# Gated mix of local attention and a gMLP on one core: absolute sums over 1024 elements, two sums over x moved into the first exponential's wait, spatial products one tile later

## Chip, core and metric

The kernel runs on one core of a Trainium2 chip. The metric is the device time of one execution in microseconds (us). A core has five engines with a queue of instructions each: PE (matrix products), ACT (elementwise functions, copies, also out of PSUM), DVE (elementwise work on tensors, also out of PSUM), POOL (little work here) and SP (issues most DMAs). Every engine works its own queue in order; between engines, and towards DMAs, an instruction waits on semaphores.

## What is computed

x has 2048 rows of 1024. With `g = sigmoid(x · gate_w)` for each row, the output is `g·a + (1-g)·b`:

```
qkv = x @ wqkv                      # 32 heads of 32
a   = softmax over 8 keys at distances 0,2,..,14 of q·k, times v, @ wo
z   = gelu(x @ w_in)                # 3584 columns: z1 | z2
z2  = layernorm(z2)
b   = (z1 * (w_sp @ z2 + b_sp)) @ w_out
```

All inputs are bf16. 

## The kernel before

Five stages follow each other on PE, and PE's instructions are in the same order from the first to the last in both kernels. (1) Columns of z2 (`z2_tile`, line 302). (2) q, k and v (`plain_rows`, line 617, and `row_pair`, line 637); they go through DRAM. (3) The rest of z2, then z1 with its gelu (line 802). (4) The spatial product `w_sp @ z2`: `g_chunk` (line 829) for two column chunks of 14 tiles each, then `seven_products` (line 920), seven times, for the other half. (5) The output products with w_out and wo (lines 1048, 1127 and 1137).

`row_pair`, `seven_products` and `both_pairs` compute a two by two block product with seven products in place of eight (the scheme of Strassen and Winograd). It needs sums of blocks, which DVE makes: `x_sums[0..3]` from x (`x_block_sums`, lines 561 to 566), `t1..t4` from w_sp (`t_sums`), `sums[0..3]` from z2 (`s_sum`). These sums are kept in fp16, and scaled by powers of two so that they do not overflow. The powers come from sums of absolute values or maxima: `q_abs`, `row_sums`, and three that the change touches:

- line 412, over the attention output `obuf` at each of four stores (`store_o`): eight sums of 512 elements a partition, into `o_l1`;
- line 1016 (`v_sum`), over the products z1·g of the two chunks: 28 sums of 512, into `v_l1`;
- line 1012 (`u_sums`), over those of the other half: 28 sums of 512, into `u_l1`.

Each is an ACT instruction `Abs` with an accumulated output; the profile shows it as an ACTIVATE and an ACTIVATION_READ_ACCUMULATOR.

In `seven_products(n)` PE makes seven products of eight matmuls each, which this text counts 0 to 6. Between them ACT copies: line 943 (bank `pa` to bank `pb`, after product 0; product 2 needs it), 945 (`e5`, after product 1), 951 (`pb` to `pc`, after product 2; product 4, which writes `pb` again, waits for it), 777 twice (seeds of two banks for the next n), 956 (after product 3), 980 (after product 6). `extra(n, place)` hangs further work between the products: `v_sum` three times at place 1 and three times at place 5. `u_sums(n-1)` stands behind line 956.

In `g_chunk` PE makes a tile of 512 columns in 16 matmuls; ACT copies it into one of three slots `gsb` (line 833), and DVE multiplies it into `z1c` (line 836).

The attention itself runs on DVE beside PE, from stage 2 to the end of `g_chunk`: for each of 8 groups of heads the products q·k and their folds (lines 348 to 362), the largest of a window (`soft_a`, lines 369 to 375), the exponential on ACT (line 378), its sum and quotient (`soft_b`), and the products with v (lines 391 to 398) of the group before, which stand in the wait for the exponential. Group 0 has no group before it.

The order of the queues is written out when the program is built. `Beat` keeps a clock of PE's work (`beat.now`) and a heap of work that is due at a time (`beat.at`); `attention_steps` yields DVE steps with a time and a duration each. `beat.run` advances the clock after each product and issues what has become due. So the times in the code (lags, durations) only set places in the queues; on the chip an instruction starts when its queue and its semaphores let it. `top`, `top_b` and lines 494 to 513 (`whole_power`) turn a maximum into a power of two: a transposition on PE (line 503), a maximum on DVE (504), a broadcast on PE (506).

Of the kernel before, what the change touches and what calls it, by code (L numbers as in the profile page):

```python
# [10 lines left out]
F32 = mybir.dt.float32  # L11
# [4 lines left out]
P = 128  # L16
# [6 lines left out]
NG = NH // HG  # L23
# [34 lines left out]
def kernel(  # L58
# [64 lines left out]
    b_in = sm.tile([P, 8], BF, name="b_in")  # L123
    b_up = sm.tile([P, 8], BF, name="b_up")
    w_l1 = sm.tile([P, 7], F32, name="w_l1")
    v_l1 = s1[:, 0:28]
    u_l1 = sm.tile([P, 28], F32, name="u_l1")
    top = sm.tile([P, 1], F32, name="top")
    top_i = sm.tile([P, 1], I32, name="top_i")
    top_b = sm.tile([P, 1], BF, name="top_b")  # L130
# [269 lines left out]
    def load_qk(g):  # L400
        sync.dma_start(q_t, bass.AP(tensor=q_d.tensor, offset=q_d.offset + g * S * C, ap=[[NJ * C, P], [1, NJ * C]]))
        sync.dma_start(k_t, bass.AP(tensor=k_d.tensor, offset=k_d.offset + (g * (S + 16) + 2) * C, ap=[[NJ * C, P], [1, NJJ * C]]))
# [4 lines left out]
    def store_o(g):  # L407
        dst = o_d[:, (g - 1) * C:(g + 1) * C].rearrange("(p j) c -> p j c", j=NJ)
        sync.dma_start(dst, obuf)
        lag = 1.5 if g + 1 == NG else 12.0  # L410
        for k in range(8):
            beat.at(beat.now + lag + 1.8 * k, lambda k=k: nc.scalar.activation(  # L412
                abs_out.rearrange("p (j c) -> p j c", j=2), obuf[:, 2 * k:2 * k + 2, :], ACT.Abs,
                accum_out=o_l1[:, 4 * g - 4 + k:4 * g - 3 + k]))

    def attention_steps(t):
        beat.at(t - 11.0, lambda: load_qk(0))
        beat.at(t + 32.0, lambda: load_v(0))
        for g in range(NG):
            for took, fn in qk_steps(0) + qk_steps(1) + [(0.73, to_two), (0.73, to_one)]:  # L420
                yield t, took, fn
            t = beat.vector
            if g + 1 < NG:
                beat.at(t + 1.0, lambda g=g: load_qk(g + 1))
            if g == 0:
                t += 3.0
            else:
                for took, fn in pv_steps(g - 1, 0):
                    yield t, took, fn
                t = beat.vector  # L430
            yield t, 1.75, soft_a
            t = beat.vector
            beat.at(t + 1.0, soft_exp)
            if g == 0:
                t += 5.0
            else:
                for took, fn in pv_steps(g - 1, 1):
                    yield t, took, fn
                t = beat.vector
                if g + 1 < NG:  # L440
                    beat.at(t + 1.0, lambda g=g: load_v(g))
                else:
                    load_v(g)
                if g % 2 == 0:
                    beat.at(t + 1.5, lambda g=g: store_o(g - 1))
            yield t, 2.25, soft_b
            t = beat.vector
        for took, fn in pv_steps(NG - 1, 0) + pv_steps(NG - 1, 1):
            yield t + 5.0, took, fn
        t = beat.vector  # L450
        beat.at(t + 9.0, lambda: store_o(NG - 1))
# [104 lines left out]
    def x_block(half, e):  # L556
        return x_even_odd[:, 4 * half:4 * half + 4, :, e]

    def x_block_sums():
        v = nc.vector  # L560
        nc.scalar.activation(a22s, x_block(1, 1), ACT.Copy, scale=x_by)
        v.tensor_scalar(a21s, x_block(0, 1), x_by, None, ALU.mult)
        TT(x_sums[0], a22s, a21s, ALU.add)
        v.scalar_tensor_tensor(x_sums[2], x_block(0, 0), x_by, a21s, ALU.mult, ALU.subtract)
        v.scalar_tensor_tensor(x_sums[1], x_block(0, 0), x_by, x_sums[0], ALU.mult, ALU.subtract)
        v.scalar_tensor_tensor(x_sums[3], x_block(1, 0), x_by, x_sums[1], ALU.mult, ALU.add)

    def q_abs(k):
        nc.scalar.activation(abs_1024.rearrange("p (k c) -> p k c", k=KT), wg_slots[4 + k // 4][:, k % 4], ACT.Abs,
# [25 lines left out]
        next(q_steps)  # L595

    QK_US = NJ * KT * 2 * C * BEAT
    beat.steps = attention_steps(beat.now + QK_US + 13.0)

    def store_rows(st, ch, j0, nj, pos0, pos1):  # L600
        for pos in range(pos0, pos1):
# [209 lines left out]
            load_z1c(0)  # L811

    gs = [0]

    def g_chunk(c):
        wsp = wsp_slots[c]
        z1c = z1c_slots[c % 2]
        for f in range(NF):
            ps = seeded.pop(0)
            n = NF * c + f + AHEAD  # L820
            if n < 2 * NF:
                seed(bsp_bc[:, 512 * (n // NF):512 * (n // NF) + 512])
            elif n == 2 * NF:
                TT(bsp_more, bsp_bc[:, 1536:2048], bsp_bc[:, 1024:1536], ALU.subtract)
                beat.on_vector(0.7)
            elif n == 2 * NF + 3:
                seed_group()
            for i in range(16):
                nc.tensor.matmul(ps[:], z2[:, f, i, :], wsp[:, i, :, :].rearrange("p a t -> p (a t)"),  # L829
                                 start=False, stop=(i == 15), skip_group_check=True)  # L830
            gsb = gsb_slots[gs[0] % 3]
            gs[0] += 1
            nc.scalar.copy(gsb, ps[:])
            if c == 1 and f == NF - 1:
                t_sums(2)
            TT(z1c[:, f, :], gsb, z1c[:, f, :], ALU.mult)
            beat.on_vector(0.43)
            beat.run(16 * 512)

    def u_late(f):  # L840
        return u_first[:, f // 7] if f % 7 == 0 else z2[:, f - 1, 0:8, :]
# [49 lines left out]
    def t_sums(k):  # L891
        if k == 0:
            TT(t1, b_hi[:, 0:8], b_lo[:, 0:8], ALU.subtract)
        elif k == 1:
            TT(t3, b_hi[:, 8:16], b_hi[:, 0:8], ALU.subtract)
        elif k == 2:
            TT(t2, b_hi[:, 8:16], t1, ALU.subtract)
        else:
            TT(t4, b_lo[:, 8:16], t2, ALU.subtract)
        beat.on_vector(2.3)  # L900
# [31 lines left out]
    def seven_products(n, extra):  # L932
        fa, fb = n, n + 7
        for f in (fa, fb):
            sync.dma_start(u_late(f).rearrange("p (c a) q -> p c (a q)", c=2),
                           z1_d[2:4, :, f * 512:(f + 1) * 512].rearrange("c p t -> p c t"))
        more = n + 1 < 7
        e5 = e5_slots[n % 2]
        extra(n, 0)
        pa, pe = seeded.pop(0), seeded.pop(0)  # L940
        product(pa, z2[:, fa, 0:8, :], lambda k: b_lo[:, k])
        pb = bank()
        nc.scalar.copy(pb[:], pa[:])
        product(pe, sums[0], lambda k: t1[:, k])
        nc.scalar.copy(e5, pe[:])
        if more:
            s_sum(n + 1, 0)
        extra(n, 1)
        product(pb, sums[1], lambda k: t2[:, k])
        pc = bank()  # L950
        nc.scalar.copy(pc[:], pb[:])  # L951
        if more:
            seed_group()
        product(pa, z2[:, fa, 8:16, :], lambda k: b_lo[:, 8 + k])
        gsb = next_gsb()
        nc.scalar.copy(gsb, pa[:])
        if n:
            u_sums(n - 1)
        g_out(fa, 2, gsb)
        extra(n, 2)  # L960
        product(pb, sums[2], lambda k: t3[:, k])
        gsb = next_gsb()
        TT(gsb, pb[:], e5, ALU.add)
        beat.on_vector(0.7)
        g_out(fb, 3, gsb)
        extra(n, 3)
        product(pc, sums[3], lambda k: b_hi[:, 8 + k])
        if more:
            s_sum(n + 1, 2)
        gsb = next_gsb()  # L970
        TT(gsb, pc[:], e5, ALU.add)
        beat.on_vector(0.7)
        g_out(fa, 3, gsb)
        extra(n, 4)
        product(pb, z2[:, fb, 8:16, :], lambda k: t4[:, k])
        if more:
            s_sum(n + 1, 1)
            s_sum(n + 1, 3)
        gsb = next_gsb()
        nc.scalar.copy(gsb, pb[:])  # L980
        g_out(fb, 2, gsb)
        extra(n, 5)
# [22 lines left out]
            TT(w_t(f, 3), b21, w_t(f, 1), ALU.subtract)  # L1005
        beat.on_vector(0.43)

    def u_sums(n):
        for h, f in enumerate((n, n + 7)):
            for k in range(2):  # L1010
                c = 4 * n + 2 * h + k
                nc.scalar.activation(abs_out.rearrange("p (i q) -> p i q", i=4), u_late(f)[:, 4 * k:4 * k + 4, :], ACT.Abs,  # L1012
                                     accum_out=u_l1[:, c:c + 1])

    def v_sum(c, f):
        nc.scalar.activation(abs_out, z1c_slots[c][:, f, :], ACT.Abs, accum_out=v_l1[:, 14 * c + f:14 * c + f + 1])  # L1016

    def u_rows(q, r, half):
        if q < 4:
# [192 lines left out]
    def extra(n, place):  # L1212
# [8 lines left out]
        if place == 0:  # L1221
            for f in sum_sets.get(n, ()):
                for k in range(4):
                    w_sum(f, k)
        if place in (1, 5) and n < 5:
            for f in range(3 * n, min(14, 3 * n + 3)):
                v_sum(place // 4, f)
        if n == 5 and place == 0:
            nc.vector.tensor_reduce(top[:], v_l1, AX.X, ALU.max)
            next(v_steps)  # L1230
        if (n, place) in ((5, 3), (6, 0)):
            next(v_steps)
        if n == 2 and place == 5:
            nc.vector.tensor_reduce(top[:], o_l1[:], AX.X, ALU.max)
            next(o_steps)
        if (n, place) in ((3, 3), (4, 0)):
            next(o_steps)
# [41 lines left out]
    beat.at(t0 + 48.0, lambda: (nc.vector.tensor_reduce(top[:], wo_l1[:], AX.X, ALU.max), next(wo_steps)))  # L1279
    g_chunk(0)  # L1280
    g_chunk(1)
    for n in range(7):
        seven_products(n, extra)
    beat.flush(1e9)
# [2 lines left out]
    prepare(1)  # L1287
    mix_pair(0)
    wo_scale(1)
    u_sums(6)  # L1290
    for k in range(4):
        wo_sum(k)
    attn_pair(0)
# [37 lines left out]
```

## Time and profile before

| | |
|---|---|
| median of 3 runs | 690.11 us (689.65 to 690.2) |
| the profiled execution, its own time | 689.57 us |
| its span, first to last instruction | 687.4 us |
| PE busy | 679.3 us, 99% of the span |
| DVE busy | 564.6 us, 82% |
| ACT busy | 425.4 us, 62% |
| granted PE clock | 1.00 in every slice |

One execution is recorded; the 2.2 us between its time and its span lie before the first and after the last instruction. In the views "idle before" is the time that an engine stood still ahead of an instruction, and the arrow names what released it. A matmul of 512 columns is recorded as 379 ns, and the next one starts 216 ns after it: they overlap.

### The profile page before, as it was taken

What the parts mean: (1) busy time and instruction counts of PE and PEld (TensorE: products, weight loads), DVE (VectorE), ACT (ScalarE), POOL (GpSimd) and SP (SyncE); (2) the same over time, 40 slices, a digit from 0 to 9 for tenths busy, and PEclk for the clock granted to TensorE, in tenths of its full rate; (3) what the DMA queues carried; (4) which work ended last, traced back from release to release, by engine and by line L of the source; (5) the groups of instructions that cost most, each with busy time, mean ns of one, the idle gap of its engine ahead of it and who ended that gap; (6) DMA issues with size and microseconds to landing.
All of it is one profiled execution on the core that took longest, in us unless ns stands there. A gap on an engine that the chain in (4) does not pass through costs nothing.

```text
span 687.4 us, 9089 instructions
## 1 busy us (share of the span) xinstructions
PE 679.3 (99%) x3327; PEld 355.3 (52%) x3327; DVE 564.6 (82%) x701; ACT 425.4 (62%) x823; POOL 13.2 (2%) x45
## 2 busy tenths in 40 slices
PE   9999999999999999999999999999899999999997
PEld 4489666666654655444444444444344444444443
DVE  4649959999999997999998889994478888776653
ACT  4458767655566999759754997327987552223332
POOL 0000000000000022000000000000000000000000
PEclk9999999999999999999999999999999999999999
DMA  8995976554597308899978999918211413222210
GB/s 234 183 198 154 203 204 151 154 130 102 157 254 202 130 1 216 191 292 346 301 255 282 147 266 236 252 36 260 77 37 56 143 42 92 62 62 71 68 45 32
DMA packets 187996, 108.67 MB, mean 158 GB/s; under 512 B 146480, under 2 KB 172592, under 8 KB 187696
## 3 DMA queue, kind: packets, MB, share of 16 engines
q1 hardware_dynamic: 186224, 101.81, 57.1%
q10 hardware_dynamic: 1728, 6.29, 2.9%
q8 instruction: 26, 0.43, 0.2%
q14 instruction: 18, 0.15, 0.1%
HBM read 59.51 MB, written 34.41 MB: 137 GB/s over the span
## 4 chain that ended last, share of the span: by engine, by line
PE 95%; ACT 3%; DMA 1%; issue 0%; SPq 0%; DVE 0%; DVEq 0%; ACTq 0%
PE ps L617 16%; PE ps L302 14%; PE ps L829 14%; PE ps L802 14%; PE ps L1048 12%; PE ps L920 10%; PE ps L637 7%; PE ps L1137 6%; ACT arena L1016 1%; PE ps L1127 1%; ACT arena L412 1%; DMA arena<-in_B_w_in_dram 1%; ACT arena L1012 0%; PE po L506 0%; ACT ps L777 0%
## 5 line engine op out<-in xcount | busy, mean ns | idle before, releaser
L617 PE MATMUL ps<-arena 128*128 128x512 bf16 (+1 forms) x640 | 115.8, 337 | 0.0
L302 PE MATMUL ps<-arena 128*128 128x512 bf16 (+1 forms) x512 | 97.7, 353 | 0.2
L829 PE MATMUL ps<-arena 128*128 128x512 bf16 x448 | 97.7, 379 | 0.0
L617 PEld LDWEIGHTS <-arena 128*128 128x128 bf16 x640 | 83.1, 144 | 27.9 <-issue 0.5
L802 PE MATMUL ps<-arena 128*128 128x512 bf16 x448 | 97.0, 379 | 0.0
L1048 PE MATMUL ps<-arena 128*128 128x512 f16 (+1 forms) x392 | 92.8, 379 | 0.0
L920 PE MATMUL ps<-arena 128*128 128x512 bf16 (+1 forms) x392 | 85.9, 379 | 3.3 <-ACT ps L951 1.7
L302 PEld LDWEIGHTS <-arena 128*128 128x128 bf16 x512 | 50.1, 98 | 47.6 <-DVE arena L322 0.3
L348 DVE TENSOR_TENSOR arena<-arena 128x8192 bf16<-128x8192 bf16 x16 | 70.7, 4422 | 0.2
L802 PEld LDWEIGHTS <-arena 128*128 128x128 bf16 x448 | 43.7, 98 | 52.4
L391 DVE TENSOR_TENSOR arena<-arena,att_A 128x8192 bf16<-128x8192 bf16 x16 | 70.7, 4419 | 0.0
L829 PEld LDWEIGHTS <-arena 128*128 128x128 bf16 x448 | 43.5, 98 | 52.5 <-issue 0.5
L920 PEld LDWEIGHTS <-arena 128*128 128x128 bf16 (+1 forms) x392 | 38.0, 98 | 49.8 <-issue 4.4
L1048 PEld LDWEIGHTS <-arena 128*128 128x128 f16 (+1 forms) x392 | 38.3, 98 | 46.1
L623 ACT CAST arena<-ps 128x512 bf16<-128x512 f32 (+1 forms) x80 | 38.3, 508 | 32.1 <-PE ps L617 30.6
L351 DVE TENSOR_TENSOR arena<-arena 128x4096 bf16<-128x4096 bf16 (+1 forms) x32 | 56.2, 1755 | 0.8
L637 PE MATMUL ps<-arena 128*128 128x512 f16 (+1 forms) x224 | 52.4, 379 | 0.0
L307 ACT ACTIVATE arena<-ps 128x512 bf16<-128x512 f32 x64 | 34.2, 537 | 27.8 <-PE ps L302 27.8
L1137 PE MATMUL ps<-arena 128*128 128x512 f16 (+3 forms) x200 | 50.3, 375 | 0.0
L1117 DVE SCALAR_TENSOR_TENSOR arena<-ps,g_s,arena 128x512 bf16<-128x512 f32 (+2 forms) x33 | 24.0, 734 | 28.7 <-ACT arena L1169 19.9
L805 ACT ACTIVATE arena<-ps 128x512 bf16<-128x512 f32 x56 | 32.3, 599 | 20.4 <-PE ps L802 19.3
L637 PEld LDWEIGHTS <-arena 128*128 128x128 f16 (+1 forms) x224 | 32.2, 144 | 16.1
(204 smaller groups left out, 789.0 us busy)
## 6 DMA issues: line engine op xcount, KB each, us to landing
arena<-k_d SPq DMA_DIRECT2D x8, 960.0 KB, 7.0
arena<-v_d SPq DMA_DIRECT2D x8, 960.0 KB, 6.6
arena<-in_A_wqkv_dram SPq DMA_DIRECT2D x24, 256.0 KB, 4.9
z_d<-arena SPq DMA_DIRECT2D x12, 512.0 KB, 7.2
arena<-q_d SPq DMA_DIRECT2D x8, 512.0 KB, 3.8
o_d<-arena SPq DMA_DIRECT2D x4, 1024.0 KB
arena<-in_B_w_in_dram SPq DMA_DIRECT2D x4, 1024.0 KB
arena<-in_B_w_sp_dram ACTq DMA_DIRECT2D x8, 512.0 KB, 6.5
```

The lines of the kernel that those rows point to most:

```text
L302: nc.tensor.matmul(ps[:, 0:N], xT[:, kt, i * P:(i + 1) * P], w2[c][:, kt, 0:N], start=(kt == 0), stop=(kt == KT - 1))
L348: TT(prod.rearrange("p (w j c) -> p w j c", w=W, j=8, c=C), in0, in1, ALU.mult)
L351: return lambda: TT(pv[:, :, 0:half], pv[:, :, 0:half], pv[:, :, half:2 * half], ALU.add)
L391: TT(prod.rearrange("p (w j d h) -> p w j d h", w=W, j=8, d=DH, h=HG), in0, in1, ALU.mult)
L617: nc.tensor.matmul(ps[:, n0:n1].rearrange("p (t c) -> p t c", c=C), lhsT, wgt[:, pos0:pos1, kt, :], start=(kt == 0), stop=(kt == KT - 1))
L623: nc.scalar.copy(slot[:, j % 4, n0:n1], ps[:, n0:n1])
L637: nc.tensor.matmul(dst[:].rearrange("p (t c) -> p t c", c=C), lhs(k), rhs[:, :, k, :], start=first and k == 0, stop=k == 3, skip_group_che ...
L802: nc.tensor.matmul(ps[:], w1[:, kt, (f % 4) * P:(f % 4 + 1) * P], xT[:, kt, 512 * c:512 * (c + 1)], start=(kt == 0), stop=(kt == KT - 1))
L829: nc.tensor.matmul(ps[:], z2[:, f, i, :], wsp[:, i, :, :].rearrange("p a t -> p (a t)"), start=False, stop=(i == 15), skip_group_check=True)
L920: nc.tensor.matmul(dst[:], lhs[:, k, :], rhs(k), start=False, stop=k == 7, skip_group_check=True)
L1048: nc.tensor.matmul(dst[:], lhs[:, j, :], rhs(j), start=first and j == 0, stop=j == 6, skip_group_check=not first)
L1137: nc.tensor.matmul(dst, lhs[:, k, :], rhs[:, k, :], start=first and k == 0, stop=k == 3, skip_group_check=not first)
```

## The change

1. *Wider sums.* `v_sum` and `u_sums` take 1024 elements in one instruction in place of 512 (14 each in place of 28), and the last `store_o` takes four sums of 1024 in place of eight of 512; they write to `abs_wide` in place of `abs_out`. The other three stores keep eight sums of 512. `v_sum` stands once at each of the places 1, 3 and 5; `u_sums(n-1, 0)` stands behind line 956 and `u_sums(n-1, 1)` behind product 5.
2. *Two sums over x.* The sums `x_sums[1]` and `x_sums[3]` leave `x_block_sums` and become two steps of the attention, behind `soft_a` of group 0. The made-up pauses of 3 and 5 us there go, and the attention's first step is due 2 us earlier, its first load at the same time as before.
3. *Spatial products one tile later.* In `g_chunk` the DVE product of a tile is issued after the copy of the next tile.

```
@@ store_o
-        for k in range(8):
-            beat.at(beat.now + lag + 1.8 * k, lambda k=k: nc.scalar.activation(
-                abs_out.rearrange("p (j c) -> p j c", j=2), obuf[:, 2 * k:2 * k + 2, :], ACT.Abs,
+        w = 4 if g + 1 == NG else 2
+        for k in range(16 // w):
+            beat.at(beat.now + lag + 0.9 * w * k, lambda k=k: nc.scalar.activation(
+                (abs_wide if w == 4 else abs_out).rearrange("p (j c) -> p j c", j=w), obuf[:, w * k:w * k + w, :], ACT.Abs,
@@ attention_steps
-        beat.at(t - 11.0, lambda: load_qk(0))
+        beat.at(t - 9.0, lambda: load_qk(0))
...
-            if g == 0:
-                t += 3.0
-            else:
+            if g:
                 for took, fn in pv_steps(g - 1, 0):
...
             if g == 0:
-                t += 5.0
+                yield t, 4.5, x_sum_1
+                yield t, 4.5, x_sum_3
+                t = beat.vector
@@ x_block_sums
-        v.scalar_tensor_tensor(x_sums[1], x_block(0, 0), x_by, x_sums[0], ALU.mult, ALU.subtract)
-        v.scalar_tensor_tensor(x_sums[3], x_block(1, 0), x_by, x_sums[1], ALU.mult, ALU.add)
+
+    def x_sum_1():
+        nc.vector.scalar_tensor_tensor(x_sums[1], x_block(0, 0), x_by, x_sums[0], ALU.mult, ALU.subtract)
+
+    def x_sum_3():
+        nc.vector.scalar_tensor_tensor(x_sums[3], x_block(1, 0), x_by, x_sums[1], ALU.mult, ALU.add)
@@
-    beat.steps = attention_steps(beat.now + QK_US + 13.0)
+    beat.steps = attention_steps(beat.now + QK_US + 11.0)
@@ g_chunk
             nc.scalar.copy(gsb, ps[:])
-            if c == 1 and f == NF - 1:
-                t_sums(2)
-            TT(z1c[:, f, :], gsb, z1c[:, f, :], ALU.mult)
+            if unmixed:
+                unmixed.pop()()
+            unmixed.append(lambda dst=z1c[:, f, :], gsb=gsb: TT(dst, gsb, dst, ALU.mult))
@@ seven_products
         if n:
-            u_sums(n - 1)
+            u_sums(n - 1, 0)
...
         extra(n, 4)
+        if n:
+            u_sums(n - 1, 1)
         product(pb, z2[:, fb, 8:16, :], lambda k: t4[:, k])
@@ u_sums, v_sum
+    def u_sums(n, h):
+        nc.scalar.activation(abs_wide.rearrange("p (i q) -> p i q", i=8), u_late(n + 7 * h), ACT.Abs,
+                             accum_out=u_l1[:, n + 7 * h:n + 7 * h + 1])
+
+    def v_sum(k):
+        nc.scalar.activation(abs_wide.rearrange("p (f t) -> p f t", f=2), z1c_slots[k // 7][:, 2 * (k % 7):2 * (k % 7) + 2, :],
+                             ACT.Abs, accum_out=v_l1[:, k:k + 1])
@@ extra
-        if place in (1, 5) and n < 5:
-            for f in range(3 * n, min(14, 3 * n + 3)):
-                v_sum(place // 4, f)
+        if place in (1, 3, 5) and n < 5 and 3 * n + place // 2 < NF:
+            v_sum(3 * n + place // 2)
@@ behind g_chunk
     g_chunk(1)
+    t_sums(2)
+    unmixed.pop()()
```

More of the change, by code (lines that the diff above doesn't have):

```diff
@@ L125 @@
     w_l1 = sm.tile([P, 7], F32, name="w_l1")
-    v_l1 = s1[:, 0:28]
-    u_l1 = sm.tile([P, 28], F32, name="u_l1")
+    v_l1 = s1[:, 0:NF]
+    u_l1 = sm.tile([P, NF], F32, name="u_l1")
     top = sm.tile([P, 1], F32, name="top")
@@ L813 @@
     gs = [0]
+    unmixed = []
     def g_chunk(c):
@@ L1006, in w_sum @@
         beat.on_vector(0.43)
[L1008 to L1016, printed above, removed]
+    def u_sums(n, h):
[4 more added lines that the diff above has]
+                             ACT.Abs, accum_out=v_l1[:, k:k + 1])
     def u_rows(q, r, half):
@@ L1233, in extra @@
         if n == 2 and place == 5:
-            nc.vector.tensor_reduce(top[:], o_l1[:], AX.X, ALU.max)
+            nc.vector.tensor_reduce(top[:], o_l1[:, 0:28], AX.X, ALU.max)
             next(o_steps)
@@ L1289 @@
     wo_scale(1)
-    u_sums(6)
+    u_sums(6, 0)
+    u_sums(6, 1)
     for k in range(4):
```

## The prediction

> **What bounds the kernel.** The page comes first: PE is busy 679.3 of 687.4 us, the chain that ended last is 95% PE and 3% ACT, and the granted clock is 1.00 everywhere. PE's instructions keep their number, shapes and order, so the change can only gain where PE stands still. The view of the waits on PE lists all of those:
>
> ```profile
> PE ps L920 <- ACT ps L951: 1.7, 2, 0.9
> PE ps L920 <- ACT ps L943: 1.6, 1, 1.6
> PE pw L101 <- PEq L1315: 0.8, 1, 0.8
> ```
>
> Two lines of `seven_products`, three waits, 3.3 us; the third line is the start. A matmul is recorded as 379 ns but followed after 216 ns, so each wait costs 0.163 us more than its idle time: 0.865 + 1.600 + 0.872 + 3 x 0.163 = **3.83 us**. A second way agrees: undisturbed, 56 matmuls take 12.09 us (n=0 starts at 459.09, n=1 at 471.18); n=1 lasts until 484.29 and n=2 until 499.17, which is 1.02 + 2.79 = 3.81 too much. This is the most that the change can bring.
>
> Why ACT is late there is read in the chain's section over that stretch, then in the timeline:
>
> ```profile
> 477.11 0.63 ACT L1016 ACTIVATE arena<-arena 128x512 bf16<-128x512 bf16 x1
> 477.64 0.19 ACT L1016 ACTIVATION_READ_ACCUMULATOR arena<-arena 128x1 f32 x1
> 477.86 0.63 ACT L412 ACTIVATE arena<-arena 128x512 bf16<-128x512 bf16 x1
> 478.39 0.19 ACT L412 ACTIVATION_READ_ACCUMULATOR arena<-arena 128x1 f32 x1
> 478.49 0.58 ACT L951 COPY ps<-ps 128x512 f32<-128x512 f32 x1
> ...
> 479.12 6.20 PE L920 MATMUL ps<-arena 128*128 128x512 f16 x28 [0.86 <-ACT ps L951]
> ```
>
> ACT has no gap. The copy that product 4 waits for stands behind three sums of line 1016 and one of line 412; PE starts 0.05 us after it. In the window 473 to 494 ACT is busy 20.5 of 21 us, 23 sums among it. All eight sums of the last store run between 474.5 and 493.5; before and after that stretch the same copies arrive in time.
>
> **What a sum costs.** From ACT's groups:
>
> ```profile
> L1016 ACT ACTIVATE arena<-arena 128x512 bf16<-128x512 bf16 x28 | 17.6, 630 | 0.6
> L848 ACT ACTIVATE arena<-arena 128x1024 bf16<-128x1024 bf16 x16 | 16.9, 1055 | 0.3
> L569 ACT ACTIVATE arena<-arena 128x1024 bf16<-128x1024 bf16 x8 | 8.8, 1097 | 0.0
> L1016 ACT ACTIVATION_READ_ACCUMULATOR arena<-arena 128x1 f32 x28 | 5.3, 188 | 0.0
> ```
>
> Sums in a row start 0.757 us apart (471.86, 472.62, 473.37): 0.630 plus 0.127 for reading the total. A sum of 1024 is not in this stage; line 848 is the nearest (contiguous, as here): 1.055, so a step of 1.18, against 1.51 for the two that it replaces. A copy behind a sum starts after 0.63, or 1.055. I take 1.055 and keep line 569's 1.097 for the range. [...]
>
> **Part 1, wider sums.** In n=1 and n=2 each, ten sums (7.6 us) become five (5.9); the last store's eight (6.1) become four (4.7). With about 3.5 us for the seven copies, n=1 held 15 or so sums before, some 15 us of work in 12.09. In the changed program's ACT queue two of the store's four sums come in n=0, after `v_sum` of place 3 and after line 980, and two in n=1, ahead of lines 956 and of the second `u_sums`. n=1 then carries seven sums, 8.3 + 3.5 = 11.8 us. Wait by wait (line numbers of before):
>
> - n=1, product 2 (in time by 0.06 before). Line 980 starts at 471.38, the next at 471.86; `v_sum` 1.18, the store's sum 1.055: line 943 runs 474.09 to 474.67, PE goes on 0.05 later, 474.72 against 474.63: **0.09 lost** (0.17 with 1.097 twice).
> - n=1, product 4 (lost 1.03). Only one `v_sum`, over at 476.4, stands between lines 945 and 951; product 2 ends at 476.45, line 951 starts 0.2 later and ends at 477.23; product 4 is due at 478.18: margin 0.9.
> - n=2, product 2 (lost 1.76). Second `u_sums` until 484.3, line 980 at 484.3, `v_sum`, line 943 from 485.8 to 486.4; due at 486.8: margin 0.4.
> - n=2, product 4 (lost 1.03): line 951 ends at about 489.3; due at 490.3.
>
> What is late next? Product 6 waits for DVE's line 963, by 0.28 and 0.11 us in time now; line 956, which holds DVE back, comes earlier (about 479.8 against 481.2 in n=1), so this margin grows to about 0.6. From n=3 on ACT had less to do than this even before.
>
> **Part 2, sums over x.** It works on DVE, off the path:
>
> ```profile
> 59.89 4.49 DVE L566 SCALAR_TENSOR_TENSOR arena<-arena,x_up 128x4096 f16<-128x4096 bf16 x1
> 64.29 4.42 DVE L348 TENSOR_TENSOR arena<-arena 128x8192 bf16<-128x8192 bf16 x1
> ```
>
> Without the two sums (4.48 each) DVE is free at 55.46, but the load of k (line 402, issued at 54.87, same place in SP's queue) lands at 61.66, so line 348 comes only 2.6 us earlier and `soft_a` ends at 82.85 in place of 85.45. The two sums fill DVE until 91.8, lines 594 to 499 until 92.6, and `soft_b`, 93.23 before, starts there: the attention gains 0.6 us, PE nothing. Cover: PE's line 503 needs `top_b` at 95.00, which was ready at 86.28 and is now ready at 92.6. Margin 2.4; a later landing of k costs PE what goes beyond. The earlier exponential delays only ACT copies with several us of room.
>
> **Part 3, products later.** DVE waits 6.4 us in six places for line 833; those go, and DVE is off the path, so this counts 0. Two covers get thinner. A `gsb` slot is held a tile (3.45 us) longer: the tightest one now is free at 421.91 and refilled at 426.84, so 4.93 becomes 1.48. And `t2` (line 897, 459.00 to 461.29, needed by n=0's product 2 at 462.55) moves behind one more step (line 394, 0.66): 461.95, margin 0.6. On SP the last store of `obuf` moves ahead of n=1's loads; those landed at 464.6 and are first used by DVE near 480.
>
> **Sum.** 3.83 - 0.09 = 3.74 us. Against the profiled execution: 689.57 - 3.74 = 685.83, span 683.7. That execution lies 0.54 below the median of the runs shown; from the median: **686.4 us**, 0.54% faster. A measurement of this kernel tells about 0.2% (1.4 us) from no change.
>
> **Rivals.**
>
> - *The sums still bunch.* ACT's queue is in order, so a store's sum that waits for the attention's last step (line 394, at 461.5) holds every copy behind it; the first now stands at about 467.9. [...] If all four fall into n=1 and n=2, up to three in one period give 9.4 + 3.5 = 12.9 us for 12.09, and with one ahead of a critical copy (1.18) about 2 us stay: 688.1. Against it: 6 us of room, and DVE gets earlier. Chance 0.10.
> - *A thin cover breaks and takes the gain back.* `t2` with 0.6, or `top_b` with 2.4 us of margin; DVE 3 to 5 us later than now at `t2` gives 689 to 691. For it: DVE has almost no gap from 431 to 462. Against it: both its waits there and the attention get shorter. Chance 0.07.
> - *Slower: the slot held a tile longer.* If two long DVE products (line 391, 4.42) stand ahead of a late tile product, the copy of line 833 three tiles on waits 8.84 - 1.48 = 7.4 us; line 873, the stores and loads of w_sp on SP, `t1` and `t2` follow, and PE loses 7.4 - 0.6 = 6.8: 690.1 - 3.7 + 6.8 = 693.2. It decides from 5.7 us of delay at `t2` on. One such product (4.42) costs 2.3 and leaves 688.7. Against it: in the changed queue no two of line 391 follow each other without a tile product between. Chance 0.08.
>
> Forecast 0.75. Faster by over 0.2%: forecast and bunching, 0.85; within 0.2%: 0.07; slower: 0.08. Range: no wait can shrink below nothing, so 690.11 - 3.83 = 686.3, less 0.5 for the runs' own spread and the lower profiled execution: 685.6 at the bottom; the bunching case, 688.3, at the top.
>
> **What would show it.** Right: PE's waits on lines 943 and 951 gone but for a tenth, n=1 and n=2 at 12.1 to 12.2 us, a sum of 1024 at 1.04 to 1.10 us, line 348 first at 61.7, DVE's waits on line 833 near nothing, and no new wait of PE on DVE. Wrong: a PE wait at line 503 near 95, at `t2` near 462, on seeds in `g_chunk`, or sums of the last store in n=2.

## The result, and the profile after

The changed kernel takes **693.98 us** (median of 7 runs, 691.21 to 696.58) against 689.83 of the kernel before beside it (689.57 to 690.2): 1.006 times as long, 95% interval 1.0039 to 1.0081. The forecast was 686.4. The profiled execution took 693.98 too, span 691.8.

From line 412 on, the new kernel's lines are 1 to 8 higher. Those used below, before and after: 503 and 504 (transposition in `whole_power`), 829 and 835 (tile matmuls of `g_chunk`), 833 and 839 (copy of a tile), 836 and 842 (its product on DVE), 844 and 850 (`natural`), 848 and 854 (`row_sums`), 871 and 877 (`scaled_biases`), 885 and 891 (`scale_rows`), 920 and 926 (products). In the experiments these lines shift by a few more.

All waits on PE, kernel after (us in total, times, longest):

```profile
PE po L504 <- ACT arena L839: 4.7, 1, 4.7
PE pw L101 <- PEq L1323: 0.8, 1, 0.8
PE ps L302 <- DMA arena<-in_B_w_in_dram: 0.3, 1, 0.3
```

The three waits in `seven_products` are gone, as forecast: its 392 matmuls now start within 85.84 us (467.25 to 553.09), before within 89.56 (459.09 to 548.66), 3.72 us less. In their place stands one wait of 4.7 us, at the transposition of `wo_steps` in the second half of `g_chunk`. Timeline of PE there, kernel after (start, us, instruction, idle before it):

```profile
427.49 0.38 PE L877 MATMUL pt<-ident,b_up 128*8 128x512 bf16 x1
427.80 3.63 PE L835 MATMUL ps<-arena 128*128 128x512 bf16 x16
436.16 0.27 PE L504 MATMUL po<-ident,top_b 128*1 128x128 bf16 x1 [4.73 <-ACT arena L839]
436.36 6.89 PE L835 MATMUL ps<-arena 128*128 128x512 bf16 x18
```

Behind the wait, 18 matmuls take 6.89 us; at 0.216 each they would take 4.1. The windows around it say why (the columns: stretch, its length, PE busy and instructions, granted clock, DMA share, GB/s):

```profile
431.43:435.30 3.87, 0.00 (x0) 1.00 0.87 317
435.30:436.16 0.86, 0.00 (x0) 0.50 0.83 338
436.16:442.13 5.97, 5.97 (x15) 0.50 0.83 176
442.13:445.00 2.87, 2.87 (x14) 1.00 1.22 262
```

The clock was halved for 6.83 us, the first 0.86 of them still within the wait. Behind it 13 matmuls came 0.40 to 0.43 us apart, and with the steps at the two ends of the stretch 2.88 us were lost against the same matmuls before. So the difference between the two profiled executions adds up: 0.48 us late from the first tile on (0.3 of it is the wait on the first load of w_in), 4.80 for the wait (the transposition's step took 5.11 in place of 0.31), 2.88 for the clock, minus 3.72: 4.44, and the spans differ by 4.4.

Why is the copy of line 839 late? The chain of work that ended last, read over this stretch (start, us, what), leads from it back to a DMA:

```profile
381.19 5.50 DMA arena<-in_B_w_sp_dram
386.71 0.33 ACTq L850
...
398.46 0.20 ACT arena L854
398.87 0.17 DVE row L860
...
434.62 0.34 ACTq L892
435.17 0.36 issue
435.53 0.59 ACT arena L839
436.16 0.27 PE po L504
```

The row sums on ACT (line 854) were late; `row_powers` on DVE waited 5.3 us for them (its first step started at 398.68, at 391.56 before); ACT's row scalings, which stand ahead of the copy, started at 422.31 in place of 417.77, behind an exponential that DVE, late itself, let go only at 420.78. The lateness itself begins at 379, in ACT's timeline:

```profile
378.57 0.59 ACT L839 CAST arena<-ps 128x512 bf16<-128x512 f32 x1 [2.38 <-PE ps L835]
384.90 0.34 ACTq L850 DMA_DIRECT2D arena<-in_B_w_sp_dram  x1
385.28 1.06 ACT L854 ACTIVATE arena<-arena 128x1024 bf16<-128x1024 bf16 x1 [6.12 <-DMA arena<-in_B_w_sp_dram]
```

In the kernel before the same load and the row sum came right behind the copy:

```profile
378.11 0.34 ACTq L844 DMA_DIRECT2D arena<-in_B_w_sp_dram  x1
378.58 1.06 ACT L848 ACTIVATE arena<-arena 128x1024 bf16<-128x1024 bf16 x1
```

In the changed kernel ACT stands 6.12 us, and not for the data of that row sum: the next thing in its queue is the *issue* of the seventh natural load (line 850), and that waits. (The chain above ends at the eighth, issued at 386.71, which waited in the same way behind the row sum.)

**What it waits for** is not in the code, but in the program built from it. There each DMA of SP and ACT has one of eight completion semaphores, handed out in turn along the planned order of all of them by the builder, and before a semaphore is used again, the program lets the issuing engine wait until the DMA that had it, eight places before, has landed. Before, the seventh load has its semaphore from the third natural load. In the changed program parts 2 and 3 move a few DMAs past each other (no natural load is edited): the seventh load comes two places later in this order and the fifth transposition of w_sp two places earlier, so the load now has its semaphore from that transposition, which SP issues at 371.26. What stands behind the load in ACT's queue waited as well: the row sum 6.12 us, and the next copy of line 839 came at 388.03 (at 381.80 before).

The landings that the traces hold fit to 0.02 us: the fifth transposition has landed at 384.88 and the seventh load is issued at 384.90, the sixth at 386.69 and the eighth load at 386.71. In e2, e3, e4, e6 and e9 to e12 below the held issue comes the same 0.02 us behind the landing of the DMA that it shares with.

### The profile page after: what moved, and what is told of

Its sections match the earlier page's. It is cut to its first block, busy times and chain, and to the rows that moved or that the text cites. A ratio compares the mean times of both kernels' runs of the same rounds, so it can differ in the third digit from the quotient of the medians.

```text
span 691.8 us, 9017 instructions
## 1 busy us (share of the span) xinstructions
PE 682.0 (99%) x3327; PEld 356.0 (51%) x3327; DVE 564.4 (82%) x701; ACT 416.4 (60%) x759; POOL 12.9 (2%) x45
## 4 chain that ended last, share of the span: by engine, by line
PE 90%; ACT 3%; DVE 3%; DMA 1%; issue 1%; SPq 0%; ACTq 0%; DVEq 0%
PE ps L622 16%; PE ps L807 14%; PE ps L302 14%; PE ps L926 12%; PE ps L1054 12%; PE ps L835 7%; PE ps L642 7%; PE ps L1143 6%; DVE arena L391 1%; ACT arena L854 1%; PE ps L1133 1%; ACT arena L891 1%; DMA arena<-in_B_w_sp_dram 1%; DMA arena<-in_B_w_in_dram 1%; ACT arena L839 1%
## 5 line engine op out<-in xcount | busy, mean ns | idle before, releaser
L835 PE MATMUL ps<-arena 128*128 128x512 bf16 x448 | 100.6, 387 | 0.0
L807 PE MATMUL ps<-arena 128*128 128x512 bf16 x448 | 97.0, 379 | 0.0
```

The costliest lines, as they stand in the source:

```text
L807: nc.tensor.matmul(ps[:], w1[:, kt, (f % 4) * P:(f % 4 + 1) * P], xT[:, kt, 512 * c:512 * (c + 1)], start=(kt == 0), stop=(kt == KT - 1))
```

## The experiments

**Theory S**: the shared semaphore holds ACT, and ACT reaches PE where PE needs a bank that the newest copy frees. **Rival D**: the deferred products hold the copies (line 839 waited 0.67 us for a late product at 426). **Rival X**: the exponential, one tile earlier in ACT's queue, held it (2.56 us at 418). In the table, "shares with" is read from the built program (the last two natural loads, or those that ACT stood for); waits are of the profiled execution; "tr" is a transposition of w_sp, 5 the fifth.

| kernel | natural load shares with | ACT stands until | PE waits for ACT near 380 to 445 | median, us |
|---|---|---|---|---|
| before | 7: load 3, 8: load 5 | - | - | 690.0 |
| after | 7: tr 5, 8: tr 6 | 385.3 (6.1) | 4.7 | 693.98 |
| e1 | as before | - | - | 686.17 |
| e2 | 6: tr 5, 8: tr 6 | 381.7 (6.2) | 3.5 | 692.16 |
| e3 | 5: a load of v, 6: a store of obuf | 380.6 (11.8) | 3.2 | 692.50 |
| e4 | 5: a load of v, 7: tr 5 | 389.3 (6.3 and 13.6) | 1.3, 3.8, 2.9 | 697.89 |
| e5 | none (in this program GpSimd's DMAs have eight others) | - | - | 686.06 |
| e6 | as after | 390.4 (11.6) | 3.8 | 693.56 |
| e9 | 7: a store of obuf, 8: tr 5 | 382.4 (3.0) | 0.9 | 689.06 |
| e10 | 7: load 4, 8: load 5 | 388.9 (2.3) | 1.3 | 690.02 |
| e11 | 7: tr 5 | 386.3 (0.3) | - | 690.20 |
| e12 | second tiny load: a store of obuf, 8: tr 7 | 390.4 (4.7 and 3.5) | 1.0, 5.3 | 697.98 |

**e1, the sums alone.** The kernel before with `v_sum`, `u_sums` and the last `store_o` as in the change, nothing else.

> Part 1 alone (the wider absolute sums) on the kernel before. All theories agree that this part is not what costs: 689.8 - 3.7 = 686.1 us (685.8 to 686.6), no wait of PE at line 504, n=1 and n=2 of seven_products at 12.1 to 12.2 us. In this kernel's program no natural load of ACT (line 850) shares its completion semaphore with a transposition of w_sp just ahead of it. If it comes out above 688, part 1 itself makes ACT late and all the theories below are wrong.

686.17 us (685.72 to 686.45, ratio 0.9938, interval 0.9921 to 0.9955). Waits on PE:

```profile
PE pw L101 <- PEq L1316: 0.8, 1, 0.8
PE ps L302 <- DMA arena<-in_B_w_in_dram: 0.7, 1, 0.7
```

Only the start and a load of w_in are left. Part 1 brings what the forecast gave the whole change; parts 2 and 3 take it away.

**e2, without the sums over x.** Parts 1 and 3 (the edits of `x_block_sums` and `attention_steps` undone).

> Parts 1 and 3, without part 2 (the two sums over x stay ahead of the attention). Theory S (shared semaphores): in the program the sixth natural load now stands eight DMAs behind the fifth transposition of w_sp and waits until that has landed; ACT stands for 5 us or more near 379, the copy of line 839 behind line 504's transposition is late by 4 to 6 us, 692 to 697 us. Rival D (the deferred products of part 3 hold the slots and the copies): the same time, but ACT's long idle stretch near 380 ends on DVE and not on a DMA of SP. Rival X (part 2's earlier exponential stands at the head of ACT's queue near 418): gone here, 686.1.

692.16 us (691.16 to 693.77). The wait near 380 ends on SP's transposition, PE waits 3.5 us at line 504, and 12 matmuls follow at half clock. Rival X is out: without its part the loss stays. Part 3 is enough to turn the rotation.

**e3 and e4, natural loads earlier.** In the changed kernel, one number:

```
-        beat.at(t0 + 2.5 * r, lambda r=r: natural(r))
+        beat.at(t0 + 1.0 * r, lambda r=r: natural(r))      # e4: 1.5 * r
```

> All three parts, the natural loads due every 1.0 us in place of 2.5. Nothing else is touched, but in the program no natural load is left whose semaphore was held by a transposition of w_sp. Theory S: ACT's wait of 6.1 us near 379 and PE's of 4.7 at line 504 go, 686.3 us (685.8 to 687.5). Rivals D and X: the deferred products and the exponential are where they were, so 693 to 695.

> The same with the natural loads due every 1.5 us: they come almost as early, but the seventh is again eight DMAs behind the fifth transposition of w_sp. Theory S: ACT stands until that has landed, near 385, and PE waits 4 to 5 us at line 504: 692 to 696. If it is the hour of the loads and not the shared semaphore, it comes out with the run at 1.0 us, near 686.3. Rivals D and X: 693 to 695.

e3: 692.50 us (689.28 to 693.97), where 686.3 was expected; e4: 697.89 (693.78 to 703.77), worse than 692 to 696. I had looked for transpositions alone; in e3 ACT stood 11.8 us in a row at two issues, at the fifth load until a load of v had landed at 373.4 and at the sixth until the store of `obuf` (line 409, issued at 370.0) had landed at 379.7. PE lost its 3.2 us there and then, at the transposition of the first half of `g_chunk` near 382; the one of the second half was in time. So the expectation was wrong, and the mechanism wider: here a load of v and a store held ACT as the transpositions did. The pair can't decide between the theories by its times.

**e5, loads issued by GpSimd.** ACT issues none of them any more:

```
     def natural(r):
-        nc.scalar.dma_start(nat_slots[r], wsp_v[8 + r])
+        nc.gpsimd.dma_start(nat_slots[r], wsp_v[8 + r])
```

> All three parts; the eight natural loads are issued by GpSimd in place of ACT, so ACT issues no DMA before its stores of w_sp and can't stand at one. Theory S: ACT has no wait on a DMA between 365 and 400, line 504 is in time, 686.3 us (685.8 to 688). If the deferred products (rival D) or the exponential (rival X) hold ACT, or if the loads land too late for the row sums whoever issues them, 692 or more.

**686.06 us** (685.84 to 689.31; ratio 0.9952, interval 0.9937 to 0.9968), with all three parts in it, deferred products and early exponential included. ACT's timeline at the place of the wait:

```profile
379.05 0.59 ACT L839 CAST arena<-ps 128x512 bf16<-128x512 f32 x1 [2.37 <-PE ps L835]
379.54 1.06 ACT L854 ACTIVATE arena<-arena 128x1024 bf16<-128x1024 bf16 x1
```

The row sum follows the copy at once, and line 504 is in time. Rivals D and X are out: what they blame is still there, and it costs nothing. The profiled execution was the one of 689.31: DVE waited there for a load on SP near 450, and PE 2.8 us for `t2` (line 903), the thin cover of 0.6 us that the prediction had named (e10 lost 2.1 us there without the change). The other five runs were 685.84 to 686.45.

**e6, the transposition later.** `next(wo_steps)` due at `t0 + 74` in place of `t0 + 66`.

> All three parts; only the transposition of wo_steps (line 504) comes 8 us of plan later (due t0+74 in place of t0+66). The DMAs keep their order, so ACT stands 6 us near 379 as in the changed kernel. Theory S with its last link (PE notices ACT's lateness only where a transposition takes the bank that the newest copy frees): PE has no wait above 1 us, no matmul at half clock, 686.2 to 688 us. If ACT's lateness reaches PE by the seeds or another way too, 690 or more.

693.56 us (693.36 to 695.12), not 686 to 688: the last link was drawn too narrow. Waits on PE:

```profile
PE pt L877 <- ACT arena L839: 3.8, 1, 3.8
PE ps L926 <- ACT arena L1021: 1.7, 1, 1.7
```

Line 504, two tiles later, no longer waits. In this execution ACT stood 11.6 us instead of 6.1, and the other extra product of this stage, line 877, one tile ahead of where 504 was, met a late copy in its turn. So it is not one instruction: each of these extra products takes the bank that the copy just ahead frees. Where ACT is late enough, moving one exposes the next.

**e7 and e8, ACT held on purpose.** The kernel before, with 2 or 5 idle activations ahead of the copy for line 503; their output isn't used:

```
+            if c == 1 and f == 3:
+                for _ in range(2):                          # e8: 5
+                    nc.scalar.activation(abs_wide, bsp_bc[:, 0:1024], ACT.Abs)
             nc.scalar.copy(gsb, ps[:])
```

> The kernel before, with two absolute values of 1024 elements (1.055 us each, results unused) on ACT right ahead of the copy of line 833 that frees the bank for line 503's transposition near 431. In the kernel before that copy ends 0.05 us before PE needs it. Clock theory: PE stands 2.0 us, too short for the clock to fall, all matmuls after it at 216 ns: 689.9 + 2.05 = 692.0 us. Rival (each us of such a wait costs 1.6, as 7.7 / 4.9 in the changed kernel): 693.2. If the margin isn't 0.05, less.

> The same with five of them. Clock theory: PE stands 5.2 us, then 8 to 16 matmuls at 427 ns in place of 216, 1.7 to 3.4 us more: 696.8 to 698.5, with a spread between runs of 2 us or more, as in the changed kernel and not in the kernel before. Without the clock: 695.1.

e7: 692.30 us (691.45 to 693.52, ratio 1.0031, interval 1.0019 to 1.0042); PE stood 1.97 us, and its step to line 503 grew by 2.04, for two activations of 1.055: the copy had no margin to give. e8: 697.58 (696.65 to 697.93); PE stood 5.23 us and 11 matmuls followed at half clock, 2.4 us. The time is as expected, the spread of 2 us or more did not come (1.3). That 2 us are too short for the clock was my estimate, shown by no run until then, and held in part. By the granted clock of each execution, five of e7's seven (0.999 or 1.0) went without a halved stretch and took 691.45 to 692.41; two (0.997) had one, if the profiled one of them speaks for both, and took 693.46 and 693.52. Windows of the profiled execution, the one of 693.46:

```profile
432.00:434.00 2.00, 0.90 (x5) 1.00 0.66 266
434.00:437.00 3.00, 3.00 (x9) 0.50 0.54 112
```

A few matmuls at full clock, then seven at half and a slower step at each end: 1.7 us lost.

**e9, without the late products.** Parts 1 and 2 (`unmixed` undone).

> Parts 1 and 2, the tile products in their old place. In this program the seventh natural load shares its semaphore with the store of obuf (line 409) and the eighth with the fifth transposition of w_sp; the eighth stands two sums (2.3 us) later in ACT's queue than the seventh, so ACT is late by some 1 to 5 us instead of 6. Theory S: 686.2 plus 0 to 5, most likely near 688 to 690, with a wait of ACT on a DMA of SP near 380. Rival D (part 3 alone is to blame): 686.2, ACT without such a wait.

689.06 us (687.23 to 695.15), inside the expected band. ACT's wait of 3.0 us near 380 is on SP's store of `obuf`, PE lost 0.9 us at line 504 in the profiled execution. So part 2 alone also turns the rotation, to a milder place.

**e10 and e11, the same without the change.** The kernel before with the loads due every 3.0 and 3.5 us.

> The kernel before with the natural loads due every 3.0 us in place of 2.5; in its program none of them shares a semaphore with a transposition of w_sp issued shortly before. Theory S: as before, 690 us (689.5 to 691).

> The kernel before with the natural loads due every 3.5 us; nothing of the change is in it, but the seventh load is now eight DMAs behind the fifth transposition of w_sp. Theory S: ACT stands 4 us or more near 380, PE waits at line 503 near 431 (or at line 871 near 427), with matmuls at half clock after it: 694 to 698 us. If the new wait were a matter of the change's own instructions, or of DMAs landing late as such, it comes out with the run at 3.0, near 690.

e10: 690.02 us (689.42 to 696.01), as expected in the median; but three of the ten runs took 692.3 to 696.0, and the profiled one, 693.99, shows the wait without any transposition in it:

```profile
ACT arena L848 <- DMA arena<-in_B_w_sp_dram: 2.3, 1, 2.3
PE po L503 <- ACT arena L833: 1.3, 1, 1.3
```

The eighth load shares with the fifth, as in the kernel before. The fifth, issued at 375.42, landed at 388.41, and ACT stood 2.3 us at the eighth for it; the issue came at 388.43.

e11: 690.20 (689.54 to 697.34), a miss. The sharing was there: load 7 was issued at 385.88, right after tr 5 landed at 385.86. But due so late it stands behind four row sums, and ACT was at work until 385.9: its gap was 0.3 us. So the price here was the landing of the partner (385.86) less the time at which ACT came to the issue (385.9), next to nothing, and not the sharing as such.

**e12, four tiny loads.** The kernel before; ACT issues four loads of 64 bytes ahead of the seventh natural load.

```
     def natural(r):
+        if r == 6:
+            for t in spare:                                 # four tiles of 8x4 bf16
+                nc.scalar.dma_start(t[:], bass.AP(tensor=B_b_sp.tensor, offset=B_b_sp.offset, ap=[[P, 8], [1, 4]]))
```

> The kernel before, with four loads of 64 bytes (not used) issued by ACT just ahead of the seventh natural load. They move nothing, but they turn the rotation of the completion semaphores: the eighth natural load now shares one with the seventh transposition of w_sp, which in the kernel before ends its issue at 398 and follows two others. Theory S: ACT stands at the eighth load from about 383 until that transposition has landed, near 390, 6 us or more, and PE waits for ACT at line 503 or 871, with matmuls at half clock after it: 695 to 700 us. If tiny loads cost only their own issue (4 x 0.35 us of ACT), below 692.

**697.98 us** (697.36 to 705.18; ratio 1.0142, interval 1.0082 to 1.0201): 256 bytes cost 8 us. ACT's timeline:

```profile
378.25 4.83 ACTq L847 DMA_DIRECT2D spare<-in_B_b_sp_dram  x4
383.12 0.36 ACTq L848 DMA_DIRECT2D arena<-in_B_w_sp_dram  x1
383.53 1.06 ACT L852 ACTIVATE arena<-arena 128x1024 bf16<-128x1024 bf16 x1 [4.70 <-DMA spare<-in_B_b_sp_dram]
...
389.96 0.36 ACTq L848 DMA_DIRECT2D arena<-in_B_w_sp_dram  x1
390.37 1.06 ACT L852 ACTIVATE arena<-arena 128x1024 bf16<-128x1024 bf16 x1 [3.51 <-DMA arena<-in_B_w_sp_dram]
```

The second of the four (it shares with the store of `obuf`, and was issued at 381.98) holds ACT 4.7 us, which was not in the expectation; the eighth natural load (with tr 7) holds it another 3.5, which was. PE then:

```profile
PE po L504 <- ACT arena L834: 5.3, 1, 5.3
```

Nothing of the change is in this kernel, and it shows the changed kernel's wait at the same place, with 13 matmuls at half clock behind it. Theory S holds.

## Why the prediction was wrong, step by step

- *Part 1, the sums.* Right, in mechanism and size. Forecast 3.74 us; `seven_products` lost 3.72 of its length, and e1 came to 686.17. A sum of 1024 takes 1.058 us here, against 1.055 taken:

```profile
L1021 ACT ACTIVATE arena<-arena 128x1024 bf16<-128x1024 bf16 x14 | 14.8, 1058 | 0.1
```

  The tenth left over is there as well: at n=1, product 2, PE's step takes 0.097 us more, forecast 0.09. Two slips in the range change nothing here: 686.3 less 0.5 is 685.8, not 685.6, and the bunching case, 688.1 in its rival, comes to the 688.3 of the range.
- *Part 2, "the attention gains 0.6 us, PE nothing".* PE got nothing, but the attention neither: the load of k landed later, line 348 started at 62.40 (61.7 forecast), and `soft_b` at 93.23, as before. Line 503 near 95 was in time, as said.
- *Part 3, "those go, and DVE is off the path, so this counts 0".* **This is one half of the step that failed.** Taken by itself the work of parts 2 and 3 does count nothing: e5, with all three, is 0.1 us from e1. What failed is the edit's side effect, put at nothing and worth 7.8 us (686.17 in e1, 693.98 with parts 2 and 3). I followed each moved DMA past its own queue (SP's) and past the transfers near it, and not through the eight semaphores it shares with ACT's DMAs.
- *"Two covers get thinner."* **The other half**: the list of covers was not complete. In the kernel before, the copy of line 833 ends at 430.83 and line 503 starts at 430.88:

```profile
430.25 0.58 ACT L833 CAST arena<-ps 128x512 bf16<-128x512 f32 x1
430.88 0.22 PE L503 MATMUL po<-ident,top_b 128*1 128x128 bf16 x1
```

  These 0.05 us are no margin. Where PE does wait for a copy, the same 0.05 lie between the copy's end and PE's start (436.11 and 436.16 in the changed kernel, and line 951 in the prediction). The margin was nothing, and this stood in the trace. ACT's own queue was waved through with "only ACT copies with several us of room". Between 380 and 431 ACT had some room, so not all of the time that it stood reached PE: 3.0 us became 0.9 in e9, 6.1 became 4.7 here, 11.6 became 3.8 in e6. In every trace in which it stood 2.3 us or more (e10), a part did.
- *Rivals.* The slower one gave 693.2, near the result by chance: it needed DVE to hold the slot, and line 839 waited 0.7 us on DVE in all. "A thin cover breaks" had the right form and the wrong covers, `t2` and `top_b`. Chances of 0.08 for slower were too low, with three parts that all reorder queues.
- *The sum* had no term for the clock: it counted a stall at its length. Here 2.88 us came on top of 4.80.

**What stays open.** When a transposition lands: tr 5, issued at 370 to 372, let its waiter go on at 381.3 (e2), 383.8 (e9), 384.9 (after), 385.9 (e11), 388.9 (e4) and 390.0 (e6); what sets this wasn't tried. With it vary ACT's wait and, likely, the spread of 691 to 697 between runs of the changed kernel. Of 66 runs of the kernel before in these comparisons two took 694.9 and 698.1, all others at most 691.2. Their granted clocks, 0.997 and 0.995 against 0.999 or 1.0, are those of the profiled executions of e7 and of the changed kernel, which had a halved stretch; a late DMA could be behind it, as e10's trace shows in small, but no trace of those two exists. Nor was it followed why the attention ran 1.5 us later than before in the gelu stage.

The best versions measured are e1 (686.17, part 1 alone) and e5 (686.06, everything, loads on GpSimd); the two can't be told apart.

## What to carry to other kernels

When an edit moves DMAs, list for each DMA issued by a *computing* engine which DMA had its completion semaphore before, and when that one lands: in the changed kernel ACT stood 6.12 us at such an issue, and with it all that was behind it in its queue. List every wait of the bounding engine by its margin, not only those that already cost something; one with nothing left turns lateness upstream into time (in e7 two activations of 1.055 us became 2.04). And where a reordering and a local gain come in one change, measure the local one alone: here it was worth 4.0 us (690.14 to 686.17), and the rest took back 7.8.

## What the runs showed of the hardware

- A stall of PE can cost more than its length, by the clock: in the changed kernel 4.80 us for the wait and 2.88 on top. From the moment at which PE stopped until the clock fell to half it took 3.87 us in the changed kernel (431.43 to 435.30), 3.34 in e8, 2.40 in e3, 2.17 in e2, 2.03 in e6, and 2.03 and 2.08 in e4. In e7 PE stood 1.97 us, and the clock fell 0.9 us after it had gone on; by the granted clocks, that wait halved it in only two of seven executions. Waits of 2.81 us in e5 and 2.09 in e10 halved nothing. So the length of the wait alone does not decide. First e6, where the clock fell 2.03 us after PE had stopped, then e5:

```profile
428.18:430.21 2.03, 0.00 (x0) 1.00 1.06 240
430.21:432.02 1.81, 0.00 (x0) 0.50 1.06 300
432.02:437.04 5.02, 5.02 (x12) 0.50 0.98 261
437.04:440.00 2.96, 2.96 (x15) 1.00 1.11 394
```

```profile
463.00:466.00 3.00, 0.67 (x4) 1.00 0.27 76
466.00:469.00 3.00, 2.53 (x12) 1.00 0.97 246
```

  What does decide was not shown. An estimate, from the times between the changes of the clock: in the changed kernel it was at half for 6.83 us and then at full for 249.17 (442.13 to 691.30, behind the last matmul), 2 and 73 times 3.413; in e4 it fell at 431.06 and 441.30, 3 times 3.413 apart. If it changes only at such steps, it may count how a wait lies to them: the 2.81 us in e5, counted back from its fall at 686.62 behind the last matmul, were parted by a step into 1.09 and 1.72. No run tried this.
- The halved stretch was longer than the wait that led to it: 6.83 us in the changed kernel, where PE had stood 4.73, and in e6, where it had stood 3.84; in e7, where PE worked all through it, 3.4. At half clock half the time is lost (matmuls 0.427 us apart in place of 0.216 in the changed kernel), so the price is at most half of what is left of the stretch when PE starts again. In the changed kernel that gives (6.83 - 0.86) / 2 = 2.98 us, measured 2.88; in e6 (6.83 - 1.81) / 2 = 2.51, measured 2.41; in e7 1.7, measured 1.69.
- ACT stood at the issue of one DMA for over 11 us (11.6 in e6, 13.6 in e4) while it had work behind it, and the profile shows this only as an idle stretch ahead of the next computation, ended by "DMA".
